# Attention and MLP in one kernel: short transposes and row sums written beside the next unit's scores, and a step that begins with its transposes

## The chip, the cores and the metric

One core of a Trainium2 chip runs the whole program. The metric is device time in microseconds (us), from launch to end; less is better. Engines are named as in the profile: PE (TensorE matmuls), PEld (its weight loads), DVE (VectorE), ACT (ScalarE), POOL (GpSimd), SP (the queue that issues nearly all transfers).

## What is computed

Attention over 4 batches and 8 heads (576 positions, head size 64) with a bias from a tiny network of the distance between positions, then a two-layer network over all 2304 tokens:

```python
scores = q @ k.T / sqrt(64) + bias[head]           # 576 x 576 for each batch and head
attn   = exp(scores - max); attn = attn / (sum(attn) + 1e-9)
x      = (attn @ v), heads side by side            # 2304 x 512
h      = maximum(x @ w_in, 0)                       # 2304 x 2048
out    = (s * h * h + b) @ w_out                    # 2304 x 512
```

All data is fp32. Scores and the two layers are made of three products each of rounded parts (hi and lo).

## The kernel before

**Stages.** First the bias of all heads is computed (until about 57 us), then attention (to about 340 us), then the MLP. The change touches attention and the seam to the MLP.

**Units and steps.** A pair is one head of two batches, x = 0 and 1, held in the two halves of the partitions; there are 16 pairs. A pair has 576 query rows a batch: four units (t = 0 to 3) of 128 rows for both batches, and a fifth (t = 4) with the last 64 rows of both in one tile, so 80 units in all. `step(n)` (L476) is one turn of a software pipeline; p, u = divmod(n, 5). In one turn stand

- **S**, the scores of unit n+2 (`scores`, L214, matmuls L228, row-tiled 64x128 in the first four units of a pair) and `biased` (L237, DVE instruction L242), which subtracts scores and bias and takes the row's minimum, once for each x;
- **T**, the transposes of unit n (`probs_t`, L287): one short one of 128 columns (L307) whose copy is on ACT (L308), then four and four long ones (L298), copied by ACT (L303) and by DVE (L305). For t = 4 they are a short one (L316, two ACT copies L318), the transposed reciprocal row sums (`norm_t`, L270, copy L272) and four long ones (L311, DVE copy L313);
- `expo` (L249), the exponentials of unit n+2 on ACT (L253), with row sums;
- **A**, the output matmuls of the pair before (`av`, L322, matmuls L332, for u = 4 L335, which then scale it on DVE, L340);
- one or two calls of `fill()` (two where u is even), each one more piece of decoding a weight tile. A tile takes five pieces: one on ACT (L372), one on POOL (L374), three on DVE (L376, L379, L382); 24 tiles are decoded here.

`norm(p)` (L263) turns the row sums of a pair into reciprocals (L265, L266) at u = 3.

**What sets the order.** Instructions of each engine run in the order in which this code issues them (`tc.manual_schedule()`). The transfers' queue SP carries at u = 4 the store of the transposed sums (L278, L280), at u = 0 their broadcast load (L285), and at n = LAST - 4 the loads of the MLP's first tokens (L410).

**Buffers.** PSUM tiles of scores come from `ps_s` (two tiles of two banks, one tile for each x; only columns 0 to 287 of each bank of 512 are written), those of transposes from `ps_t` (two tiles of one bank). Three tiles each are there for the biased scores (`tt`) and for the exponentials (`pr`).

**The seam.** At the end (L612 to L618) the last steps are woven with the splitting of the first tokens into hi and lo (`split_x`, L415: ACT L418, then DVE L419) and the first MLP blocks (`expand`, L421, matmuls L429).

## Time and profile before

| what | us |
|---|---|
| runs shown | 747.33, 746.71, 746.08 (median 746.71) |
| span of the profiled execution, first to last instruction | 747.1 |
| the profiled execution's own time, launch to end | not among the times shown; the span stands for it |
| PE busy | 716.6 (96%) |
| DVE, ACT, POOL busy | 429.3 (57%), 363.5 (49%), 186.3 (25%) |
| mean granted PE clock | 0.993 |

Read the page so: PE's busy time is nearly the span, but matmuls overlap, so a busy PE can still wait between two of them; the waits show in the weight loads (PEld) and in the starts of matmuls. The shares of DVE and ACT are means over stages: both work far more in attention than in the MLP.

### The profile page before, as it was taken

The numbers are of one execution on the slowest core, as the hardware profiler recorded it, in microseconds if no ns is written. First come the engines' busy times: TensorE is split into PE (matmuls) and PEld (weight loads), VectorE is DVE, ScalarE is ACT, GpSimd is POOL, SyncE is SP. The second block draws the span as 40 slices with busy tenths as digits, with TensorE's granted clock in tenths as the row PEclk, the third lists the DMA queues.
The fourth block names the chain that finished last, engine by engine and source line by source line (L and its number), as shares of the span: only waits on it lengthen the run. The fifth ranks groups of instructions, "written<-read, shape, count | busy, mean of one in ns | idle before, by whom it ended". The sixth has DMA issues, their size and how long they took to land.

```text
span 747.1 us, 12023 instructions
## 1 busy us (share of the span) xinstructions
PE 716.6 (96%) x4530; PEld 534.9 (72%) x4530; DVE 429.3 (57%) x794; ACT 363.5 (49%) x756; POOL 186.3 (25%) x194
## 2 busy tenths in 40 slices
PE   8978999899999999969999999999999999999998
PEld 4436666666666666646888888888888888888896
DVE  7976888788888878963288632233332332223332
ACT  7967767576666667653445322232222332222332
POOL 7991534445333234203654100000000000000000
PEclk9999999999999999989999999999999999999999
DMA  5977765556564765351012130000300002000100
GB/s 171 297 205 245 227 204 170 176 156 212 160 215 134 228 214 184 97 176 60 13 57 85 29 114 0 1 1 0 113 1 0 1 1 84 1 0 1 57 1 28
DMA packets 39817, 76.98 MB, mean 103 GB/s; under 512 B 9040, under 2 KB 12368, under 8 KB 39760
## 3 DMA queue, kind: packets, MB, share of 16 engines
q1 hardware_dynamic: 39616, 75.90, 32.4%
q8 instruction: 35, 0.57, 0.3%
q10 hardware_dynamic: 144, 0.33, 0.1%
q14 instruction: 22, 0.18, 0.1%
HBM read 55.45 MB, written 20.13 MB: 101 GB/s over the span
## 4 chain that ended last, share of the span: by engine, by line
PE 81%; issue 3%; POOL 3%; ACT 2%; DVE 1%; DMA 1%; SPq 1%; DVEq 0%; ACTq 0%; POOLq 0%
PE hps L429 27%; PE o L453 27%; PE sps L228 8%; PE xps L332 7%; PE tps L298 7%; PE xps L335 2%; PE tps L307 2%; PE tps L311 1%; POOL kr L204 1%; ACT ptr L318 1%; DMA x<-xt 1%; POOL qr L204 1%; PE tps L270 1%; POOL full L374 0%; PE tps L316 0%
## 5 line engine op out<-in xcount | busy, mean ns | idle before, releaser
L453 PE MATMUL o<-who,gt 128*128 128x512 f32 x576 | 192.5, 393 | 0.0
L429 PE MATMUL hps<-x,whi 128*128 128x512 f32 (+1 forms) x640 | 184.5, 373 | 0.0
L434 DVE SCALAR_TENSOR_TENSOR r<-r,sb 128x512 f32<-128x512 f32 (+1 forms) x80 | 56.7, 708 | 193.2 <-ACT r L433 193.2
L433 ACT ACTIVATE r<-hps 128x512 f32<-128x512 f32 (+1 forms) x80 | 44.4, 555 | 227.5 <-PE hps L429 227.5
L429 PEld LDWEIGHTS hps<-x,whi 128*128 128x128 f32 x640 | 117.5, 189 | 24.1 <-issue 0.4
L453 PEld LDWEIGHTS o<-who,gt 128*128 128x128 f32 x576 | 108.3, 188 | 24.1
L429 PE MATMUL hps<-x,wli 128*128 128x512 f32 (+1 forms) x320 | 119.0, 372 | 0.0
L253 ACT ACTIVATE pr<-tt,mn 128x576 f32<-128x576 f32 x144 | 110.1, 767 | 10.3 <-DVE mn L242 9.7
L453 PE MATMUL o<-wlo,gt 128*128 128x512 f32 x288 | 113.2, 393 | 0.0
L242 DVE CUSTOM_DVE_ANT_0 tt<-sps,bt 128x576 f32<-128x576 f32 x128 | 91.6, 753 | 29.4 <-PE sps L228 24.0
L228 PEld LDWEIGHTS sps<-kr,qr 64*128 64x128 f32 (+1 forms) x864 | 67.8, 185 | 39.6 <-issue 10.1
L228 PE MATMUL sps<-kr,qr 64*128 64x288 f32 (+1 forms) x864 | 88.3, 311 | 5.8 <-POOL kr L204 2.7
L439 DVE SCALAR_TENSOR_TENSOR gt<-r,sb,gt 128x512 fp32r<-128x512 f32 (+1 forms) x80 | 56.3, 704 | 54.0 <-ACT gt L438 54.0
L438 ACT ACTIVATE gt<-r,sb 128x512 fp32r<-128x512 f32 (+1 forms) x80 | 54.4, 680 | 52.2 <-DVE r L434 52.2
L298 PE MATMUL tps<-ident,pr 128*128 128x128 f32 x512 | 77.1, 282 | 0.3 <-ACT ptr L308 0.3
L332 PE MATMUL xps<-pt,vt 128*64 128x288 f32 x512 | 76.5, 421 | 0.0
L429 PEld LDWEIGHTS hps<-x,wli 128*128 128x128 f32 x320 | 60.3, 188 | 11.1
L298 PEld LDWEIGHTS tps<-ident,pr 128*128 128x128 f32 x512 | 57.7, 142 | 11.4 <-ACT ptr L308 11.2
L453 PEld LDWEIGHTS o<-wlo,gt 128*128 128x128 f32 x288 | 54.2, 188 | 11.6
L374 POOL TENSOR_SCALAR full<-full 128x512 f32<-128x512 f32 x32 | 22.6, 705 | 115.1 <-ACT full L372 114.6
L332 PEld LDWEIGHTS xps<-pt,vt 128*64 128x64 f32 x512 | 31.5, 137 | 24.3 <-issue 10.6
L136 PE MATMUL bps<-f,pt__110 128*32 128x512 f32 x288 | 42.8, 599 | 5.3 <-POOL f L119 2.2
(69 smaller groups left out, 748.1 us busy)
## 6 DMA issues: line engine op xcount, KB each, us to landing
bias<-stg SPq DMA_DIRECT2D x36, 288.0 KB
raw<-in_moe_w_in_dram SPq DMA_DIRECT2D x16, 512.0 KB
raw<-in_moe_w_out_dram SPq DMA_DIRECT2D x16, 512.0 KB
bt<-bias SPq DMA_DIRECT2D x7, 1152.0 KB
qt<-in_q_dram SPq DMA_DIRECT2D x16, 320.0 KB
kt<-in_k_dram SPq DMA_DIRECT2D x16, 320.0 KB
vt<-in_v_dram SPq DMA_DIRECT2D x16, 320.0 KB
rb<-rs SPq DMA_DIRECT2D x32, 144.0 KB
```

The source lines that it names most:

```text
L136: nc.tensor.matmul(pb[32 * c:32 * c + 32, 0:512], w2bd, fs[c][0][:, 0:8], start=True, stop=True)
L228: nc.tensor.matmul(o, a, b, start=(i == 0), stop=(i == 2))
L242: nc.vector.tensor_tensor_reduce(tt.rearrange("p (a b) -> p a b", a=2), ps[x][:, :, 0:HALF], bias.rearrange("p (a b) -> p a b", a=2), -1.0 ...
L253: nc.scalar.activation(pr[:, x], tts.pop((n, x)), AF.Exp, bias=mn[:, x:x + 1], scale=-1.0, accum_out=sums[p][:, col:col + 1])
L298: nc.tensor.transpose(ps[:, 128 * kb:128 * kb + 128], pr[:, part, 64 * part + 128 * kb:64 * part + 128 * kb + 128], ident)
L332: nc.tensor.matmul(ps[64 * x:64 * x + 64, hf, 0:HALF], vt[:, 4 * x + kb, :], pt[:, kb, x, c], start=(kb == 0), stop=False)
L429: nc.tensor.matmul(ps[:, 0:n], w[0, g][:, a, fc], xs_t[c, a][:, j, 0:n], start=(i == 0), stop=(i == 3 * KB - 1))
L433: nc.scalar.activation(r, ps[:, 0:n], AF.Relu)
L434: nc.vector.scalar_tensor_tensor(r, r, sb[:, 0:1], r, op0=ALU.mult, op1=ALU.mult)
L438: nc.scalar.activation(hi, r, AF.Identity, bias=sb[:, 1:2])
L439: nc.vector.scalar_tensor_tensor(lo, r, sb[:, 1:2], hi.bitcast(F32), op0=ALU.add, op1=ALU.subtract)
L453: nc.tensor.matmul(os_t[c][i], gt[:, a, tok], w[1, g][:, fo], start=(f == 0 and j == 0), stop=(f == NF - 1 and j == 2))
```

## The change

A step now begins with T, then S, then A. The short transposes no longer take a tile of `ps_t`: they write columns 288 to 415 of the x = 0 score tile of unit n+1 (`spare`), of its first bank, and for t = 4 the row sums go to the same columns of its second bank. Only in the last units, where there is no such tile, a `ps_t` tile is used. `norm_t` becomes `norm_copy`, with its transpose moved up beside the other short one. The exponential of x = 1 of a unit is issued one step later, between the short copy and the first long copy of that step (`later`). `norm(p)` keeps its place behind `biased`, now in the step's second half.

```diff
@@ -266,10 +266,9 @@
         nc.vector.reciprocal(su, su)
         rows[p] = su
 
-    def norm_t(p, ps):
-        nc.tensor.transpose(ps[0:9, 128:256], rows.pop(p), ident)
+    def norm_copy(p, ps):
         rt = sm.tile([9, 128], F32, tag="rt", name="rt", bufs=2)
-        nc.vector.tensor_copy(rt, ps[0:9, 128:256])
+        nc.vector.tensor_copy(rt, ps)
         rts[p] = rt
 
     def norm_store(p):
@@ -284,40 +283,53 @@
         for x in range(2):
             nc.sync.dma_start(out=rbs[p][64 * x:64 * x + 64, :], in_=rs_d[p][x:x + 1, :].broadcast_to([D, S]))
 
-    def probs_t(n, part):
+    def spare(n):
+        if n + 1 < LAST - 1:
+            return units[n + 1][2][0][:, :, HALF:]
+        return ps_t.tile([128, 512], F32, tag="t", name="tps").rearrange("p (a b) -> p a b", a=2)
+
+    def probs_t(n):
         p, t = divmod(n, 5)
         pr = units[n][0]
         if p not in pts:
             pts[p] = (ptp.tile([128, 4, 2, S], F32, tag="pt", name="pt"),
                       ptp.tile([128, S], F32, tag="ptr", name="ptr"))
         pt, ptr = pts[p]
-        ps = ps_t.tile([128, 512], F32, tag="t", name="tps")
         c = slice(128 * t, 128 * t + 128)
-        if t < 4 and part < 2:
-            for kb in range(4):
-                nc.tensor.transpose(
-                    ps[:, 128 * kb:128 * kb + 128],
-                    pr[:, part, 64 * part + 128 * kb:64 * part + 128 * kb + 128], ident)
-            o, i = pt[:, :, part, c], ps.rearrange("p (a b) -> p a b", a=4)
-            if part == 0:
-                nc.scalar.activation(o, i, AF.Copy)
-            else:
-                nc.vector.tensor_copy(o, i)
-        elif t < 4:
-            nc.tensor.transpose(ps[:, 0:128], pr.rearrange("p x j -> p (x j)")[:, 512:640], ident)
-            nc.scalar.activation(ptr[:, c], ps[:, 0:128], AF.Copy)
-        elif part == 0:
+        end = spare(n)
+        if t < 4:
+            nc.tensor.transpose(end[:, 0, 0:128], pr.rearrange("p x j -> p (x j)")[:, 512:640], ident)
+            nc.scalar.activation(ptr[:, c], end[:, 0, 0:128], AF.Copy)
+            later(n + 1)
+            for x in range(2):
+                ps = ps_t.tile([128, 512], F32, tag="t", name="tps")
+                for kb in range(4):
+                    nc.tensor.transpose(
+                        ps[:, 128 * kb:128 * kb + 128],
+                        pr[:, x, 64 * x + 128 * kb:64 * x + 128 * kb + 128], ident)
+                o, i = pt[:, :, x, c], ps.rearrange("p (a b) -> p a b", a=4)
+                if x == 0:
+                    nc.scalar.activation(o, i, AF.Copy)
+                else:
+                    nc.vector.tensor_copy(o, i)
+        else:
+            nc.tensor.transpose(end[0:64, 0, 0:128], pr[:, 0, 512:S], ident)
+            nc.tensor.transpose(end[0:9, 1, 0:128], rows.pop(p), ident)
+            ps = ps_t.tile([128, 512], F32, tag="t", name="tps")
             for kb in range(4):
                 nc.tensor.transpose(
                     ps[:, 128 * kb:128 * kb + 128], pr[:, 0, 128 * kb:128 * kb + 128], ident)
+            for x in range(2):
+                nc.scalar.activation(
+                    ptr[64 * x:64 * x + 64, 512:S], end[0:64, 0, 64 * x:64 * x + 64], AF.Copy)
+            later(n + 1)
+            norm_copy(p, end[0:9, 1, 0:128])
             nc.vector.tensor_copy(
                 pt[:, :, :, 512:S], ps.rearrange("p (a x b) -> p a x b", a=4, x=2))
-        else:
-            nc.tensor.transpose(ps[0:64, 0:128], pr[:, 0, 512:S], ident)
-            for x in range(2):
-                nc.scalar.activation(
-                    ptr[64 * x:64 * x + 64, 512:S], ps[0:64, 64 * x:64 * x + 64], AF.Copy)
-            norm_t(p, ps)
+
+    def later(n):
+        if (n, 1) in tts:
+            expo(n, 1)
 
     def av(p, kb, hf):
         h, b0 = pairs[p]
@@ -477,6 +489,8 @@
         p, u = divmod(n, 5)
         m = n + 2
         cur = 0 <= n < LAST
+        if cur:
+            probs_t(n)
         if ok(m, 0):
             scores(m)
             biased(m, 0)
@@ -484,13 +498,8 @@
             biased(m, 1)
         if cur and u == 3:
             norm(p)
-        if cur:
-            for part in (2, 0, 1) if u < 4 else (1, 0):
-                probs_t(n, part)
         if ok(m, 0):
             expo(m, 0)
-        if ok(m, 1):
-            expo(m, 1)
         if p >= 1:
             av(p - 1, u, 0)
             av(p - 1, u, 1)
@@ -549,7 +558,7 @@
         26: ((load_bias, 0, 2, 3),),
         33: ((scores, 0), (biased, 0, 0), (expo, 0, 0), (biased, 0, 1)),
         35: ((expo, 0, 1), (scores, 1), (biased, 1, 0),
-             (expo, 1, 0), (biased, 1, 1), (expo, 1, 1), (load_w, *early[0]), (load_w, *early[1]),
+             (expo, 1, 0), (biased, 1, 1), (load_w, *early[0]), (load_w, *early[1]),
              (load_q, 2), (load_k, 2), (load_v, 1)),
     }
     for st in range(STEPS):
```

Three places show the order that results; "waits" names the semaphores (engine counters or transfers) that an instruction waits for.

PE, from A of a step with u = 3 to the transposes of the next pair's u = 0, somewhere in the middle of attention; before:

```order
L332 MATMUL xps<-pt,vt 64x288 x4
L228 MATMUL sps<-kr,qr 128x288 [waits DVE_49] x2
L228 MATMUL sps<-kr,qr 128x288 x10
L316 MATMUL tps<-ident,pr 64x128 [waits Activation_49]
L270 MATMUL tps<-ident,su 9x128 [waits DVE_49,Activation_49]
L311 MATMUL tps<-ident,pr 128x128 [waits DVE_49]
L311 MATMUL tps<-ident,pr 128x128 x3
L335 MATMUL xps<-ptr,vt 128x288 x2
L228 MATMUL sps<-kr,qr 128x288 [waits DVE_49] x2
L228 MATMUL sps<-kr,qr 128x288 x10
L307 MATMUL tps<-ident,pr 128x128 [waits DVE_49]
```

and now:

```order
L344 MATMUL xps<-pt,vt 64x288 x4
L316 MATMUL sps<-ident,pr 64x128 [waits DVE_49]
L317 MATMUL sps<-ident,su 9x128 [waits DVE_49]
L320 MATMUL tps<-ident,pr 128x128 [waits Activation_49]
L320 MATMUL tps<-ident,pr 128x128 x3
L228 MATMUL sps<-kr,qr 128x288 [waits PE_49]
L228 MATMUL sps<-kr,qr 128x288 [waits DVE_49]
L228 MATMUL sps<-kr,qr 128x288 x10
L347 MATMUL xps<-ptr,vt 128x288 x2
L301 MATMUL sps<-ident,pr 128x128 [waits DVE_49,Activation_49]
```

The transposed sums (in: su) no longer wait for ACT, but stand right behind A of the step in which DVE makes the reciprocals, with the scores behind them. The short transpose (L301) now waits for DVE as well as ACT.

ACT, in a step in which a decode piece falls; before:

```order
L308 ACTIVATE ptr<-tps 128x128 [waits PE_49]
L303 ACTIVATE pt<-tps 128x4x128 [waits PE_49]
L253 ACTIVATE pr,su<-tt,mn 128x576 [waits DVE_49] x2
L372 ACTIVATE full_986<-raw 128x512 [waits DMAHW0_49]
L308 ACTIVATE ptr<-tps 128x128 [waits PE_49]
L303 ACTIVATE pt<-tps 128x4x128 [waits PE_49]
```

and now (two steps):

```order
L302 ACTIVATE ptr<-sps 128x128 [waits PE_49]
L253 ACTIVATE pr,su<-tt,mn 128x576 [waits DVE_49]
L312 ACTIVATE pt<-tps 128x4x128 [waits PE_49]
L253 ACTIVATE pr,su<-tt,mn 128x576 [waits DVE_49]
L384 ACTIVATE full_985<-raw 128x512 [waits DMAHW0_49]
L302 ACTIVATE ptr<-sps 128x128 [waits PE_49]
L312 ACTIVATE pt<-tps 128x4x128 [waits PE_49]
```

One exponential moved behind the short copy; the decode piece (L384) still stands ahead of the short copy of the next step.

DVE, from the reciprocals at u = 3 on; before:

```order
L265 TENSOR_SCALAR su<-su 128x9 [waits Activation_49]
L266 RECIPROCAL su<-su 128x9 [waits DVE_49]
L305 COPY pt<-tps 128x4x128 [waits PE_49]
L242 ISA tt,mn<-sps,bt 128x576 [waits PE_49]
L242 ISA mn 128x1
L242 ISA tt,mn<-sps,bt 128x576 [waits PE_49,Activation_49]
L242 ISA mn 128x1
L272 COPY rt<-tps 9x128 [waits DMAHW4_49,DMAHW3_49,PE_49]
```

and now:

```order
L265 TENSOR_SCALAR su<-su 128x9 [waits Activation_49]
L266 RECIPROCAL su<-su 128x9 [waits DVE_49]
L271 COPY rt<-sps 9x128 [waits DMAHW3_49,DMAHW4_49,PE_49,Activation_49]
L327 COPY pt<-tps 128x8x64 [waits PE_49]
L242 ISA tt,mn<-sps,bt 128x576 [waits PE_49]
L242 ISA mn 128x1
L242 ISA tt,mn<-sps,bt 128x576 [waits PE_49]
L242 ISA mn 128x1
```

The copy of the sums now waits for ACT too, and stands ahead of the biased scores of its step.

## Rows read from the trace of the kernel before

**Rows 1.** Windows view, two stretches: us, busy time of each engine, PEclk, DMA, GB/s
```profile
125.00:150.00 25.00, 23.03 (x178) 15.66 (x176) 20.81 (x44) 14.64 (x37) 10.02 (x10) 0.93 0.59 186
325.00:350.00 25.00, 18.98 (x97) 12.48 (x94) 8.54 (x15) 8.19 (x18) 1.56 (x2) 0.86 0.48 161
```

**Rows 2.** Waits view, 60 to 330 us: who waited for whom, total us, times, longest
```profile
PEld tps L298 <- ACT ptr L308: 11.2, 63, 0.5
PEld tps L270 <- ACT ptr L318: 10.9, 15, 0.7
...
PE sps L228 <- POOL kr L204: 2.7, 4, 1.3
```

**Rows 3.** Timeline, one step, PE: start us, us, engine, line, op
```profile
183.20 1.07 PE L228 MATMUL sps<-kr,qr 64*128 64x288 f32 x12
...
184.36 1.19 PE L298 MATMUL tps<-ident,pr 128*128 128x128 f32 x8
...
185.48 1.19 PE L332 MATMUL xps<-pt,vt 128*64 128x288 f32 x8
...
186.60 1.07 PE L228 MATMUL sps<-kr,qr 128*128 128x288 f32 x6
```

**Rows 4.** Timeline, end of a step with u = 3 and its u = 4
```profile
191.04 0.76 DVE L242 CUSTOM_DVE_ANT_0 tt<-sps,bt 128x576 f32<-128x576 f32 x1 [1.18 <-issue]
...
192.61 0.22 DVE L266 RECIPROCAL su<-su 128x9 f32<-128x9 f32 x1
...
193.25 1.06 PE L228 MATMUL sps<-kr,qr 64*128 64x288 f32 x12
...
194.24 0.30 PE L316 MATMUL tps<-ident,pr 128*64 128x128 f32 x1
...
194.34 0.76 DVE L242 CUSTOM_DVE_ANT_0 tt<-sps,bt 128x576 f32<-128x576 f32 x1 [0.38 <-PE sps L228]
194.57 0.44 ACT L318 ACTIVATE ptr<-tps 64x64 f32<-64x64 f32 x2 [0.82 <-PE tps L316]
...
195.07 0.28 PE L270 MATMUL tps<-ident,su 128*9 128x128 f32 x1 [0.53 <-ACT ptr L318]
...
195.19 0.60 PE L311 MATMUL tps<-ident,pr 128*128 128x128 f32 x4
...
195.62 1.14 PE L335 MATMUL xps<-ptr,vt 128*128 128x288 f32 x4
...
195.70 0.27 DVE L272 COPY rt<-tps 9x128 f32<-9x128 f32 x1
...
195.91 0.67 DVE L313 COPY pt<-tps 128x512 f32<-128x512 f32 x1
...
196.79 0.76 DVE L340 TENSOR_TENSOR rb<-xps,rb 128x576 f32<-128x576 f32 x1 [0.22 <-PE xps L335]
```

**Rows 5.** Lines view, shapes apart, whole span: line, engine, op, count, busy us, mean ns
```profile
L253 ACT ACTIVATE pr<-tt,mn 128x576 f32<-128x576 f32 x144 | 110.1, 767 | 10.3 <-DVE mn L242 9.7
...
L379 DVE SCALAR_TENSOR_TENSOR full<-raw,full 128x512 uint32<-128x512 uint32 x32 | 31.7, 989 | 0.6
...
L376 DVE TENSOR_SCALAR full<-full 128x512 uint32<-128x512 uint32 x32 | 29.5, 921 | 2.3 <-POOL full L374 2.1
...
L382 DVE SCALAR_TENSOR_TENSOR full<-raw,full 128x512 uint32<-128x512 uint32 x32 | 22.9, 717 | 0.6
...
L372 ACT ACTIVATE full<-raw 128x512 f32<-128x512 f32 x32 | 21.1, 660 | 0.0
```

**Rows 6.** Timeline, the seam from attention to the MLP
```profile
334.02 0.69 DVE L419 TENSOR_TENSOR x<-x 128x512 fp32r<-128x512 f32 x1 [1.30 <-ACT x L418]
334.37 0.09 PEld L270 LDWEIGHTS tps<-ident,su 128*9 128x9 f32 x1 [6.21 <-ACT ptr L318]
...
335.40 2.12 PE L335 MATMUL xps<-ptr,vt 128*128 128x288 f32 x4
...
341.02 3.13 PE L332 MATMUL xps<-pt,vt 128*64 128x288 f32 x24
```

## The prediction

> **What bounds the kernel now.** I read the busy times by stretch first, then who waits for whom, then one step in order of time, then the seam. In attention PE sets the pace: in a middle stretch it is busy 23.03 of 25 us, but DVE is close behind with 20.81, while late in the program there is little of DVE [rows 1]. So a wait taken off PE is worth its full length only as long as DVE and ACT can follow. The waits view shows two waits of PE that the change aims at: the fifth long transpose waits for the short copy on ACT, 63 times, 11.2 us by the weight loads, and the transposed sums wait for the copies L318, 15 times, 10.9 us [rows 2]. One step reads so [rows 3]: scores start at 183.20, the long transposes at 184.36, the output at 185.48, the next scores at 186.60. The period is 3.40 us, of which A is 1.12.
>
> **What the change removes.** Both short products leave the transposes' two buffers, so the second four need no copy on ACT.
> - Long transposes: a wait is 11.2/63 = 0.18 us by the weight loads. Part of it lies beside the matmul that still runs; hidden by one transpose (0.43/4 = 0.11, from 195.19 to 195.62 [rows 4]) it would be worth 0.07, hidden by nothing 0.18. I take 0.15, nearer to the latter because the eight take 1.12 where twice the four would take 0.86: 63 x 0.15 = **-9.5** (between -4.4 and -11.2).
> - Sums: L316 to L270 takes 0.83 (194.24 to 195.07), L270 to the next 0.12 [rows 4]; the difference of 0.71 goes, in 15 pairs: **-10.7**. The 16th is at the seam, below.
>
> A full step would then be 3.25: S 1.00, A 1.12, T 1.13. No matmul is added, and the same instructions run on ACT and DVE; what S, T and A cost by themselves is only moved, and the shape changes of PE's tile between them stay as many. SP's transfers keep their places in the step; none is passed.
>
> **What it adds.** Four waits, each worked from the start of a step's scores as time 0; the DVE bias of these scores starts at 1.09 (193.25 to 194.34 [rows 4]).
> - *Reciprocals.* At u = 3 DVE takes 1.79 from the first bias to the end of the reciprocal (191.04 to 192.61 + 0.22), so they are ready at 2.88. PE now wants them after S (0.99), A (1.12) and L316 (0.12), at 2.23. Wait 0.65, 16 times: **+10.4** [rows 3, 4]. Before, T stood ahead of A and one step later, so that this was covered.
> - *The sums' copy.* The scores behind it need the bank back: transposed sums 0.28, the two ACT copies 0.44, DVE's copy 0.27, with hand-overs of 0.06 (195.01 to 195.07) some 1.1 in all. PE has 0.12 + 0.43 and a shape change of about 0.1 to do. Wait 0.45, 16 times: **+7.2** [rows 4]. The old cover, A, now stands behind the scores.
> - *The bank that DVE reads.* The first short transpose of a step writes into the tile whose bias DVE computes, and so waits for it. DVE is free at 2.45 (195.70 - 193.25), then come the decode pieces F, then the copy of the long transposes (0.67), then the bias, wanted at 3.25 + 1.09 = 4.34: spare 1.22. The bias ends at 4.34 + 0.76 = 5.10, and PE wants it at 3.25 + 2.12 = 5.37: spare 0.27, so 1.49 together [rows 4]. Two pieces in a row are on DVE for 0, 0.92, 1.91, 1.71 or 0.72 [rows 5]. At u = 0 the excess over 1.49 is 0.42 and 0.22, 0.13 in the mean of five; at u = 4 the scaled output (0.76) comes on top, excess 0.19, 1.18 and 0.98, mean 0.47; at u = 2 there is only one bias to compute and nothing is over. 15 x 0.60 = **+9.0** (0 if DVE's pieces run at the short ends of their times, 18 if they meet the long ones each time).
> - *The short copy behind a decode piece.* The bias ends at 1.85, the exponential (0.77 [rows 5]) at 2.67, the short copy at 2.95, scores follow at 3.25: spare 0.25 with a hand-over. A decode piece of ACT of 0.66 between them [rows 5] makes 0.41, 24 times 9.8; half of these fall in steps already held up by one of the other waits: **+4.9** (0 to 9.8).
>
> The moved exponential itself costs nothing: it runs while PE transposes, and its unit is wanted a step later; without that cover it would be 0.77 on the path.
>
> **The seam.** Before, the last L270 waits 6.21 us for two ACT copies queued behind the splitting of the first tokens, and then PE runs slow: four output matmuls take 2.12 from 335.40 where they took 1.14 [rows 4, 6]; the clock in that stretch is 0.86, which is a part at the lower of its two levels, 1.2 GHz, after the idle time [rows 1]. Now both short transposes and the long ones go ahead of those copies. The first MLP block can start on the tokens that are there; the last split ends at 334.71, then DVE copies sums (0.27) and transposes (0.67) and scales (0.76): 336.4, when the output steps that started at 341.02 can start: **-4.5** (0 if the tokens land later, -6.3 with nothing behind the split).
>
> Scores wait for POOL's rounded keys 2.7 us before [rows 2]; a slower pace gives POOL time, I take half: **-1.3**.
>
> Sum: -9.5 - 10.7 + 10.4 + 7.2 + 9.0 + 4.9 - 4.5 - 1.3 = **+5.5 us**. The span of the profiled execution is 747.1, 0.4 above the median of the runs shown (746.7) and inside their spread; I put the sum on the median: **752.2 us**.
>
> A rule of the Trainium skill speaks against this change: PSUM — Partial Sum Buffer, section "PSUM bank collisions raise a hardware error", says to guard PSUM by bank and group of 32 partitions, not by address, since two engines in one bank collide even in different columns. The trace agrees: before, L270 waits 0.53 for copies that read other columns of its bank [rows 4]. By columns alone the bank's wait would be nothing and the sum -3.5; by the rule it is +5.5, and the new order shows L301 waiting for DVE.
>
> **The rivals.**
> 1. *DVE and ACT keep up* (faster). If the decode pieces lie so that the short transpose finds its bank read and the copy stands free, the last two of the four waits are 0: 752.2 - 13.9 = 738.3. It decides at F = 1.49 us of DVE pieces after u = 0, and 0.73 after u = 4. For it: DVE's pieces vary, and ACT has slack (14.64 of 25 [rows 1]). Against: their mean is 0.72 to 0.99 [rows 5], and DVE's 20.81 of 25 leaves little. Chance 0.15.
> 2. *Gains and losses cancel.* The moved waits cost about what the removed ones did and the seam gives little, or the change does not shorten PE's path because the waits were beside running matmuls: 747 within 1.5. Chance 0.11.
> 3. *The clock falls more often.* In the stretch from 125 to 150 us the granted clock is 0.93, below full, in a part of attention in which scores waited for POOL; so PE that pauses can lose its full clock. A stretch like it costs 25 x 0.07 = 1.75 us. With four more of them: 752.2 + 7 = 759.2. Against: the sums' waits of 0.53 us [rows 4] recur in every pair, and this stretch, which shows the lower clock, is one with a wait for POOL of up to 1.3 [rows 2]. Chance 0.12.
>
> On the third, the skill's page TensorE: Matmul & The Clock Gate, section "HAM oscillation — how this bites in real kernels", says that waits between bursts of matmuls let the clock fall each time, so that the cost repeats. No row here shows waits of the new lengths doing so.
>
> **How the numbers follow.** The forecast itself, slower by some 3 to 9 us, has 0.62. The first rival lies on the other side, so the range reaches towards it: the lower end takes the bank's and the decode piece's waits at a third of their price and is 743; the upper end adds the decode piece in full (4.9) and a seam that gives a third (3), 760. Outside are most of the first rival and the end of the third. About 0.2% (1.5 us) is what a measurement of this kernel can tell from no change. Faster: the first rival and a little of the second, 0.18. Same: most of the second, 0.08. Slower: the forecast and the third, 0.74.
>
> **What the profile of the changed kernel would show.** Right: the waits of long transposes for the short copy gone; PE waiting at L317 for the reciprocal some 0.65 in each pair, at the scores behind it for the sums' copy or ACT, at L301 for the bias in steps after two decode pieces; pairs that take over 17 us, where five steps of 3.40 made 17.0 at most; no idle time of 6 us at the seam, and the clock full there. Wrong: pairs of 16.4 or less, L301 never waiting, or L317 finding its sums ready; or long idle stretches of PE with a clock below full in the middle of attention.

## The result and the profile after

The changed kernel takes 759.44 us (median of 4 runs, 756.43 to 760.17), the kernel before, run beside it, 747.02 (4 runs, 746.08 to 747.41): a ratio of 1.0149, with a 95% interval of 1.013 to 1.0168, so about 11 us slower where +5.5 was forecast. Three of its runs show a mean granted clock of 0.990 to 0.993, the one of 756.43 shows 0.998. The profiled execution spans 757.1 us, 10.0 more than the one of before.

Where these 10.0 us came from is read by the starts of the same instructions in the two profiled executions (us):

| instruction on PE | before | after | later by | in this stretch |
|---|---|---|---|---|
| second unit's scores, L228 | 56.61 | 59.11 | 2.50 | +2.50 |
| pair 0, the output matmuls of u = 4 (first L335, now L347) | 88.97 | 94.75 | 5.78 | +3.28 |
| pair 13, the same | 314.56 | 325.64 | 11.08 | +5.30 |
| first MLP matmul (L429, now L441) | 336.92 | 342.34 | 5.42 | -5.66 |
| last pair's u = 4 over, third MLP block begins | 349.06 | 354.56 | 5.50 | +0.08 |
| first output matmul of the MLP (L453, now L465) | 352.07 | 360.46 | 8.39 | +2.89 |
| 49th of them | 374.49 | 384.50 | 10.01 | +1.62 |

From there to the start of PE's last matmul both take 368.54 us. Thirteen pairs of attention make only half of the loss; the rest lies at the start, in the first pair, and behind the seam.

**The middle of attention.** The waits view of the changed kernel, 60 to 330 us (who waited for whom, total us, times, longest):

```profile
PEld sps L317 <- DVE su L266: 12.5, 15, 1.1
PE sps L317 <- DVE su L266: 9.7, 15, 0.9
...
PE sps L301 <- DVE mn L242: 8.3, 13, 1.0
...
PEld sps L228 <- DVE rt L271: 4.5, 15, 0.4
PEld sps L228 <- ACT ptr L302: 3.9, 18, 0.3
...
PEld sps L228 <- POOL kr L204: 0.9, 2, 0.7
PE sps L228 <- POOL kr L204: 0.4, 1, 0.4
```

The two waits of [rows 2] that the change aimed at are gone, and all four that the prediction named stand in their place: the sums' transpose for the reciprocals, the short transpose for the bias that reads its tile (8.3 us of matmuls, of which 4.9 fall in the first pair, before 88 us), the scores for the sums' copy and for the short copy. The wait for POOL's keys fell from 2.7 us of matmuls to 0.4.

The same step as in [rows 4], on PE, with ACT's and DVE's part (start us, us, engine, line, and in brackets the idle time before and what ended it):

```profile
195.70 0.32 PE L301 MATMUL sps<-ident,pr 128*128 128x128 f32 x1
195.86 1.04 PE L307 MATMUL tps<-ident,pr 128*128 128x128 f32 x8
196.82 1.06 PE L228 MATMUL sps<-kr,qr 64*128 64x288 f32 x12
197.81 1.19 PE L344 MATMUL xps<-pt,vt 128*64 128x288 f32 x8
198.93 0.30 PE L316 MATMUL sps<-ident,pr 128*64 128x128 f32 x1
199.57 0.21 DVE L266 RECIPROCAL su<-su 128x9 f32<-128x9 f32 x1
199.84 0.28 PE L317 MATMUL sps<-ident,su 128*9 128x128 f32 x1 [0.61 <-DVE su L266]
199.96 0.60 PE L320 MATMUL tps<-ident,pr 128*128 128x128 f32 x4
200.16 0.45 ACT L323 ACTIVATE ptr<-sps 64x64 f32<-64x64 f32 x2 [0.48 <-PE sps L317]
200.49 1.53 PE L228 MATMUL sps<-kr,qr 64*128 64x288 f32 x12
200.63 0.28 DVE L271 COPY rt<-sps 9x128 f32<-9x128 f32 x1 [0.30 <-ACT ptr L323]
201.95 1.24 PE L347 MATMUL xps<-ptr,vt 128*128 128x288 f32 x4
```

A step without a wait takes 3.23 (195.70 to 198.93): T 1.12, S 0.99, A 1.12. The reader should compare L316 to L317, 0.91 here, with L316 to L270 in [rows 4], 0.83: the sums' wait of before was not removed, it was exchanged for one on another engine. Behind it the scores, 0.99 in steps without a wait, take 1.46 to the next line: the copy L323 of the first short transpose waits until L317 has written the other bank of the tile, and DVE's copy of the sums then waits for L323.

**The first pair.** The timeline of the first steps of attention, where no pair stands before and so there is no A:

```profile
59.76 0.93 PE L228 MATMUL sps<-kr,qr 64*128 64x288 f32 x8
61.64 0.30 PE L301 MATMUL sps<-ident,pr 128*128 128x128 f32 x1 [0.95 <-DVE mn L242]
...
64.84 0.30 PE L301 MATMUL sps<-ident,pr 128*128 128x128 f32 x1 [1.04 <-DVE mn L242]
```

The short transpose follows the scores directly and waits about 1 us in each step for the bias that reads its tile.

**The seam.** The timeline of the changed kernel:

```profile
340.26 1.14 PE L347 MATMUL xps<-ptr,vt 128*128 128x288 f32 x4
341.66 2.63 ACT L430 ACTIVATE x<-x 128x512 fp32r<-128x512 f32 x4 [3.35 <-DMA x<-xt]
342.34 0.50 PE L441 MATMUL hps<-x,whi 128*128 128x512 f32 x1 [0.94 <-ACT x L430]
344.93 0.27 DVE L271 COPY rt<-tps 9x128 f32<-9x128 f32 x1
...
359.55 0.76 DVE L352 TENSOR_TENSOR rb<-xps,rb 128x576 f32<-128x576 f32 x1 [3.74 <-DMA rb<-rs]
360.46 0.60 PE L465 MATMUL o<-who,gt 128*128 128x512 f32 x1 [2.73 <-DVE rb L352]
```

and its chain of waits (start us, us, what) between 344.93 and 359.55:

```profile
347.09 8.54 DMA rs<-rt
...
356.25 3.18 DMA rb<-rs
```

PE no longer idles 6.21 us, and its four matmuls take 1.14 instead of 2.12 [rows 6]. But the last pair's sums are now copied at 344.93, behind the splitting of the first tokens; their way through memory and back takes until 359.5, and the first output matmul, whose PSUM the scaling L352 must leave, waits for it. In this execution the clock then drops. The windows view (us, busy time of PE, PEld, DVE, ACT, POOL, PEclk, DMA, GB/s), two stretches that answer to [rows 1], the stretch behind this wait, and the one at the start:

```profile
125.00:150.00 25.00, 22.97 (x180) 16.02 (x181) 20.69 (x48) 14.55 (x39) 7.85 (x8) 1.00 0.68 206
330.00:355.00 25.00, 22.66 (x145) 14.64 (x141) 13.19 (x26) 12.50 (x29) 1.06 (x1) 1.00 0.48 162
...
53.00:60.20 7.20, 6.56 (x51) 3.41 (x53) 1.44 (x4) 2.60 (x5) 5.21 (x5) 0.53 0.63 162
360.00:364.00 4.00, 3.54 (x9) 2.80 (x10) 2.10 (x3) 0.72 (x1) 2.34 (x2) 0.58 0.08 18
```

The full clock at the seam was forecast and is there; 0.58 behind it, most of the stretch at the lower of the two levels (1.2 GHz), was not. That the clock falls there is not certain: six profiles show PE idle for 2.0 to 2.7 us before this matmul. In four of them (the changed kernel, a_seam, a_first, a_nodec) the 48 matmuls behind it take 23.9 to 24.0 us, in a_pst and a_x1 22.4 and 22.5, as in the kernel before.

### The profile page after: what moved, and what is told of

Same layout as the page of the kernel before. It is cut to its first block, busy times and chain, and to the rows that moved or that the text cites. A ratio compares the mean times of both kernels' runs of the same rounds, so it can differ in the third digit from the quotient of the medians.

```text
span 757.1 us, 12070 instructions
## 1 busy us (share of the span) xinstructions
PE 719.2 (95%) x4530; PEld 540.7 (71%) x4530; DVE 426.9 (56%) x794; ACT 357.0 (47%) x756; POOL 184.9 (24%) x194
## 4 chain that ended last, share of the span: by engine, by line
PE 73%; DMA 10%; DVE 9%; issue 4%; ACT 2%; SPq 1%; POOL 1%; DVEq 0%; ACTq 0%; POOLq 0%
PE o L465 27%; PE hps L441 25%; PE sps L228 8%; DMA rs<-rt 5%; PE tps L307 4%; PE xps L344 4%; DVE tt L242 3%; PE bps L136 3%; DMA bias<-stg 2%; PE sps L301 1%; DMA bt<-bias 1%; DVE full L391 1%; PE xps L347 1%; DVE rb L352 1%; DMA raw<-in_moe_w_in_dram 1%
## 5 line engine op out<-in xcount | busy, mean ns | idle before, releaser
L465 PE MATMUL o<-who,gt 128*128 128x512 f32 x576 | 193.6, 395 | 2.7 <-DVE rb L352 2.7
L441 PE MATMUL hps<-x,whi 128*128 128x512 f32 (+1 forms) x640 | 183.7, 371 | 1.2 <-ACT x L430 0.9
L441 PEld LDWEIGHTS hps<-x,whi 128*128 128x128 f32 x640 | 116.9, 188 | 25.9 <-ACT x L430 1.4
L465 PEld LDWEIGHTS o<-who,gt 128*128 128x128 f32 x576 | 109.1, 189 | 27.5 <-ACT whi L405 3.1
L441 PE MATMUL hps<-x,wli 128*128 128x512 f32 (+1 forms) x320 | 118.7, 371 | 0.0
L465 PE MATMUL o<-wlo,gt 128*128 128x512 f32 x288 | 113.9, 395 | 0.0
L228 PE MATMUL sps<-kr,qr 64*128 64x288 f32 (+1 forms) x864 | 98.9, 315 | 2.8 <-ACT stg L143 0.7
L228 PEld LDWEIGHTS sps<-kr,qr 64*128 64x128 f32 (+1 forms) x864 | 72.9, 187 | 20.9 <-issue 7.4
L441 PEld LDWEIGHTS hps<-x,wli 128*128 128x128 f32 x320 | 60.1, 188 | 10.8
L307 PE MATMUL tps<-ident,pr 128*128 128x128 f32 x512 | 66.6, 273 | 0.2 <-ACT ptr L302 0.2
L465 PEld LDWEIGHTS o<-wlo,gt 128*128 128x128 f32 x288 | 54.5, 189 | 11.7
L314 DVE COPY pt<-tps 128x512 f32<-128x512 f32 x64 | 44.0, 687 | 20.3 <-PE tps L307 19.6
L136 PE MATMUL bps<-f,pt__110 128*32 128x512 f32 x288 | 44.6, 624 | 5.2 <-POOL f L119 2.3
```

Of the source, the lines that this page charges most:

```text
L136: nc.tensor.matmul(pb[32 * c:32 * c + 32, 0:512], w2bd, fs[c][0][:, 0:8], start=True, stop=True)
L228: nc.tensor.matmul(o, a, b, start=(i == 0), stop=(i == 2))
L307: nc.tensor.transpose(ps[:, 128 * kb:128 * kb + 128], pr[:, x, 64 * x + 128 * kb:64 * x + 128 * kb + 128], ident)
L441: nc.tensor.matmul(ps[:, 0:n], w[0, g][:, a, fc], xs_t[c, a][:, j, 0:n], start=(i == 0), stop=(i == 3 * KB - 1))
L465: nc.tensor.matmul(os_t[c][i], gt[:, a, tok], w[1, g][:, fo], start=(f == 0 and j == 0), stop=(f == NF - 1 and j == 2))
```

## The experiments

Times are medians; each kernel was compared with the kernel before on its own chip (747.1 to 748.4 us), and its distance to the changed kernel is the difference of their ratios to before, times 747. "Period" is the mean time of a pair: from the first L347 (L335 in before) of pair 0 to that of pair 13, divided by 13. For the kernel before it is 17.35 us in its profile, where nine pairs without a disturbance take 16.87 to 16.91, 16.89 in the middle; for the changed kernel it is 17.76.

### Where do 13.9 us of the forecast come from: the decode pieces

```diff
 def decode_w(kind, g, i):
     if g < 3:
-        full = fulls[g][:, kind, i]
+        for _ in range(5):
+            yield
+        w_full[kind, g, i] = fulls[g][:, kind, i]
+        return
...
+    for g in (2, 1):
+        nc.gpsimd.memset(fulls[g], 0.01)
```

The same edit in the changed kernel (a_nodec) and in the kernel before (b_nodec): the decoding of 24 weight tiles is left out and constants stand in their place, so that the outputs are not those of the reference.

> The changed kernel without the decoding of the weight tiles of parts 0 to 2 (24 tiles; constants stand in their place, so the first layers' results are not the reference's): the pieces of decoding leave ACT, DVE and POOL during attention, all else stays. Theory (the forecast's third and fourth added wait are made by these pieces): 9.0 + 4.9 = 14 us come off, 745 us, between 742 and 749, and the pairs in attention take 16.8 or less, while the waits for the reciprocals and for the sums' copy stay. Rival (the added waits come from the order of the step itself, the pieces only fill idle time): less than 5 us come off, 754 or more.

> The kernel before, with the same decoding left out (the same constants in its place). Theory: before the change the steps have cover for the pieces, so no more than 5 us come off (742 to 747), most of them waits for POOL's rounded keys; the difference of the two kernels without decoding is then about 0 to 5 us where it is 11 with it. Rival: the pieces cost the kernel before as much as the changed one (some 14 us, 733), and the difference stays at 11.

Measured: 747.28 us (741.55 to 749.53) for the changed kernel without decoding, ratio 0.9981 (0.9959 to 1.0003), 12.5 below it; 746.42 (744.88 to 748.03) for the kernel before without it, a ratio of 0.9977 (0.9962 to 0.9993) to before, some 1.7 us. (This second gain is partly given back in the first pair, where POOL writes the constants and a part runs at the lower clock: it is 3.6 us longer.) The periods are clearer: 16.86 and 16.92. The waits view of a_nodec, 60 to 330 us:

```profile
PE sps L317 <- DVE su L266: 9.4, 15, 0.7
...
PEld sps L228 <- DVE rt L271: 4.5, 15, 0.3
PE sps L301 <- DVE mn L242: 4.3, 5, 1.0
```

The waits for reciprocals and for the sums' copy stay as they were, to 0.3 us; the waits for the short copy on ACT (3.9 us in the changed kernel) are gone, and those of L301 for the bias fall from 13 to 5, behind the first pair from 8 (3.4 us) to 1 (0.3 us). So the two groups of added waits are told apart: without pieces of decoding the change wins 0.06 us a pair (16.92 - 16.86); the pieces cost the changed kernel 0.90 a pair (17.76 - 16.86), where (9.0 + 4.9)/16 = 0.87 was forecast, and the kernel before 0.43 (17.35 - 16.92), most of it waits for POOL's keys.

How the 0.90 divides is read from PE's starts in the 13 pairs of the period (us):

| from ... to | changed | a_nodec | more | forecast, for 13 pairs |
|---|---|---|---|---|
| A to the next T: the short transpose's wait for the bias | 77.35 | 72.83 | 4.52 | 7.8 |
| T to S | 75.94 | 76.01 | -0.07 | 0 |
| S to A: the scores' wait for the short copy | 77.60 | 70.39 | 7.21 | 4.2 |

The sum agrees, its two parts do not: the bias costs 0.35 us a pair (0.60 forecast), the short copy 0.55 (0.9 us in all of that are waits for POOL's keys). Of the 39 steps with u = 0, 2 or 4 there are 18 in which the scores take 1.33 us or more to the next line and not 0.99. Two of them wait for POOL's keys; in 16 a decode piece stands on ACT just ahead of the short copy. They pay 0.35 to 0.44 us each (forecast 0.41), but 16 of the 21 pieces in these pairs do so, where half was forecast. One of the 16, on the timeline of the changed kernel:

```profile
225.01 0.66 ACT L384 ACTIVATE full<-raw 128x512 f32<-128x512 f32 x1
225.45 1.49 PE L228 MATMUL sps<-kr,qr 64*128 64x288 f32 x12
225.57 0.26 ACT L302 ACTIVATE ptr<-sps 128x128 f32<-128x128 f32 x1
225.89 0.82 PEld L228 LDWEIGHTS sps<-kr,qr 64*128 64x128 f32 x11 [0.25 <-ACT ptr L302]
```

The decode piece on ACT stands ahead of the short copy, and the scores wait for that copy.

### The tile that is read, not the columns

```diff
-            return units[n + 1][2][0][:, :, HALF:]
+            return units[n + 1][2][-1][:, :, HALF:]
```

> The changed kernel with the spare columns in the score tile of x = 1 of unit n+1 (the one whose bias DVE computes last) in place of x = 0. Nothing else is changed. Theory (PE waits at the short transpose for DVE's reading of the bank, not of the columns): the bias of x = 1 ends 0.76 to 0.9 us later, so with a spare of 0.3 in a step without excess each of some 45 steps waits 0.3 to 0.5 longer: 10 to 22 us more than the changed kernel, 769 to 781. Rival (the wait hangs on the columns, or there is slack beyond what was counted): within 3 us of the changed kernel, 757 to 762.

Measured: 776.34 us (774.86 to 777.47), ratio 1.0374 (1.0343 to 1.0405), 16.8 above the changed kernel; period 18.90. The waits view, 60 to 330 us, and the starts of two steps on the timeline:

```profile
PE sps L301 <- DVE mn L242: 26.0, 42, 1.7
```

```profile
199.20 0.30 PE L301 MATMUL sps<-ident,pr 128*128 128x128 f32 x1 [0.61 <-DVE mn L242]
...
203.09 0.30 PE L301 MATMUL sps<-ident,pr 128*128 128x128 f32 x1 [0.61 <-DVE mn L242]
```

The columns are the same 288 to 415, free in either tile; only the tile whose bias DVE reads last is another. 26.0 us of matmul waits stand where 8.3 stood (behind the first pair 20.2 and 3.4). What a short transpose waits for is the end of a reader of other columns of its tile. Whether bank or whole tile makes the wait, this run cannot tell: the bias reads both banks of the tile. The step shown above speaks for the whole tile, since there L323 waits 0.48 us for L317 and L271 0.30 for L323, each for a neighbour in the other bank; no run tests it.

### The order alone

```diff
 def spare(n):
-        if n + 1 < LAST - 1:
-            return units[n + 1][2][0][:, :, HALF:]
```

> The changed kernel's order alone: the short transposes and the sums go to a tile of the transposes' buffers as before, all else stays as changed. Theory (the waits of the long transposes for the short copy and of the sums for theirs return, and now both stand ahead of the scores, on the path): 63 x 0.2 to 0.3 us and 16 x 0.5 to 0.7 us more, less 9 us for the bank that DVE reads, which is no longer shared; the exponential that now stands between the short copy and the first long one comes on top where the third tile waits for it: 5 to 25 us above the changed kernel, 764 to 784. Rival (the order is what costs, and the columns bring nothing): within 3 us of the changed kernel, 756 to 762.

Measured: 778.08 us (2 runs), ratio 1.04 (1.0368 to 1.0432), 18.8 above the changed kernel; period 19.10. Its waits view, 60 to 330 us:

```profile
PEld tps L305 <- ACT ptr L300: 42.2, 57, 1.6
```

The wait for the short copy, 11.2 us in [rows 2], is 42.2 in the new order (by the weight loads too, 57 times). The theory holds. The order alone is about 30 us slower than the kernel before; the columns take 18.8 of that back, which is less than the order costs. Whether the columns could be had in another order was not tried.

### Both exponentials at once

```diff
         if ok(m, 0):
             expo(m, 0)
+        if ok(m, 1):
+            expo(m, 1)
...
-            later(n + 1)
```

> The changed kernel, but both exponentials of a unit are issued together, as before; nothing is postponed. The forecast took the postponing at nothing and said that without cover it would be 0.77 us on the path. Theory (the short copy, on which the next scores wait, then stands behind both exponentials; the bias of the second ends 0.68 later and it takes 0.77): the scores of full steps wait 0.3 us and more, 48 times and over, so 10 to 25 us more than the changed kernel, 769 to 784. Rival (ACT has slack enough): within 3 us of the changed kernel.

Measured: 775.35 us (774.82 to 776.32), ratio 1.038 (1.036 to 1.04), 17.3 above the changed kernel; period 18.90. Rows of its waits view, 60 to 330 us:

```profile
PEld sps L228 <- ACT ptr L302: 16.5, 33, 1.1
PEld sps L301 <- DVE mn L242: 15.1, 29, 1.1
```

With the second exponential ahead of the short copy the scores wait four times as long for that copy. The moved exponential is a needed part of the order; that it is free where the change puts it is not shown by this run.

### The sums behind the output matmuls

```diff
-            nc.tensor.transpose(end[0:9, 1, 0:128], rows.pop(p), ident)
...
-            norm_copy(p, end[0:9, 1, 0:128])
...
             av(p - 1, u, 1)
+        if cur and u == 4:
+            norm_t(p)
```

> The changed kernel, but the transpose of the row sums and its copy stand behind the output matmuls of their step, in a tile of the transposes' own buffers. Theory (PE waits for the reciprocal in every pair, 12.5 us by the weight loads, and the scores behind it wait for the copy of the sums, 4.5 us): 7 to 13 us less than the changed kernel, 746 to 752. Rival (DVE sets the pace of a pair, so what is taken off here turns up as a longer wait of the short transposes for the bias): less than 4 us.

Measured: 751.89 us (750.09 to 754.77), ratio 1.0067 (1.0046 to 1.0087), 6.1 below the changed kernel, between what theory and rival expected; period 17.49. A row of its waits view, 60 to 330 us:

```profile
PEld tps L312 <- DVE rt L271: 10.1, 15, 0.9
```

The wait of L317 is gone, but its successor is already there: the long transposes of the next step find one of the two tiles held by the sums' copy. 0.27 us a pair is left (17.76 - 17.49, 3.5 us in 13 pairs), and the first pair, which shares the L317 wait, is 1.4 shorter. At the seam two things nearly cancel: up to the first MLP matmul 3.8 us more (20.51 against 16.70; the sums' transpose again waits for two ACT copies behind the split tokens), behind it 4.5 less (the first output matmul follows the third MLP block in 3.01 us, as in before, not in 5.90, and the next stretch takes 22.42 instead of 24.04). So the wait for the reciprocals was real, but moving the sums gives back only what the two tiles allow: neither text was right about the size.

### The first pair in the old order

```diff
-        if cur:
+        if cur and n >= 5:
             probs_t(n)
...
+        if cur and n < 5:
+            probs_t(n)
```

(with `spare` taking a `ps_t` tile for n < 5.)

> The changed kernel with the first pair (5 steps) in the order of before: scores, then transposes in the transposes' own buffers; all later steps as changed. Theory (in the first pair no output matmuls lie between scores and transposes, so each short transpose waits about 1 us for the bias of the scores just made): 2 to 4 us less than the changed kernel, and the waits of 1.3 us between scores and short transposes from 60 to 78 us gone. Rival (the slow start is the clock at its lower level from 53 to 60 us and nothing else): within 1 us.

Measured: 753.7 us (751.55 to 756.43), ratio 1.0087 (1.0067 to 1.0107), 4.6 below the changed kernel by the ratios. From the second unit's scores to L347 of pair 0 it takes 31.71 us; the changed kernel 35.64, the kernel before 32.36; the period stays at 17.76. The windows view from 60 to 80 us, of the changed kernel and of this one:

```profile
60.00:80.00 20.00, 13.33 (x123) 10.82 (x123) 12.52 (x31) 13.24 (x37) 0.00 (x0) 0.99 0.89 287
```

```profile
60.00:80.00 20.00, 18.87 (x157) 13.96 (x153) 14.89 (x37) 15.84 (x43) 3.05 (x4) 1.00 0.89 289
```

PE is busy 13.33 us of 20 in the one, 18.87 in the other. So the first pair alone costs some 4 us, a little more than expected.

### The seam, twice

```diff
-    for work in (att, xsp, xsp, xsp, xsp, att, h0, ...
+    for work in (att, att, xsp, xsp, xsp, xsp, h0, ...
```

> The changed kernel with one difference at the seam: the last unit's transposes and copies are issued before the splitting of the first tokens, not behind it. Theory (the sums of the last pair are copied late, their store and broadcast load take some 12 us, and the first matmul of the second layer waits for the scaled output behind them, 3.1 us, after which the clock stands at its lower level): 3 to 5 us less than the changed kernel, so about 754 to 756, and no idle time of 3 us before the first output matmul of the MLP. Rival (the wait there is set by the tokens or by the weights, and the loss sits in the pairs alone): within 1.5 us of the changed kernel.

Measured: 757.19 us (755.44 to 762.03), ratio 1.0142 (1.0115 to 1.0169): the same as the changed kernel, and the theory missed. A row of SP on its timeline points to the reason:

```profile
339.90 4.18 SPq L277 DMA_DIRECT2D rs<-rt  x1
```

The sums were copied earlier, but the issue of their store took 4.18 us instead of 0.49, with the issues of four weight loads of 512 KB each (L371) just ahead of it in the queue. So these were moved as well:

```diff
-    for e in late[0:4]:
-        load_w(*e)
...
+    lw = map(lambda e: load_w(*e), late[0:4])
+    for work in (att, att, lw, lw, lw, lw, xsp, xsp, xsp, xsp, h0, ...
```

> The changed kernel with the second of the last attention steps ahead of the splitting of the first tokens, and the loads of four weight tiles of 512 KB behind the store of the last sums. Theory: the store of the sums then issues at once, the broadcast row sums arrive before the first output matmul of the last pair, the wait of about 3 us in front of it and the slower clock behind it go: 4 us below the changed kernel (3 to 6), 753.5 to 756.5. Rival: the store's chain is late for another cause (the loads of the first tokens, or the late weight loads then hold up something else), and the time stays above 757.

Measured: 755.35 us (754.8 to 757.15), ratio 1.0101 (1.008 to 1.0122), 3.6 below the changed kernel. The store and the first output matmul now:

```profile
343.85 0.48 SPq L277 DMA_DIRECT2D rs<-rt  x1
...
359.53 0.47 PE L465 MATMUL o<-who,gt 128*128 128x512 f32 x1 [1.43 <-DVE rb L352]
```

The store issues in 0.48 us, the wait falls from 2.73 to 1.43, and the output matmuls behind it run at full clock (22.45 us for 48 of them, not 24.04). The theory holds, though the wait did not go altogether: in the chain of waits the load of the sums back (`rb<-rs`) now takes 5.74 us, where it took 3.18.

### All four faults undone

a_sums, a_first and a_seam2 together.

> The changed kernel with the four faults found so far undone: the sums transposed behind the output matmuls, the first pair in the order of before, the second attention step ahead of the splitting of the first tokens, the late weight loads behind the store of the sums. Theory: 6.1 + 4.6 + 4.1 us less than the changed kernel if the parts add up, less some 2 us because the sums moved and the seam mended both end the wait at the first output matmul: 13 us less, 746 (744 to 749), no better than the kernel before. Rival (the parts hide each other's waits): more than 18 us less, 741 or below, faster than before.

Measured: 747.76 us (747.05 to 749.35, 12 runs), ratio 0.9998 (0.9982 to 1.0013), 11.3 below the changed kernel. Mended at these four places, the changed order is worth as much as the order of before (period 17.49 against 17.35), as the theory had it.

### What the change aimed at, in the order of before

b_sums puts the sums' transpose of the kernel before behind the output matmuls, in a tile of its own; b_best takes the seam of a_seam2 as well.

```diff
-            norm_t(p, ps)
...
             av(p - 1, u, 1)
+        if cur and u == 4:
+            norm_t(p)
```

> The kernel before with the sums' transpose behind the output matmuls alone. Theory: 5 to 9 us below the kernel before; the rows of the wait for the copies of L318 go and the pairs take 16.3 us instead of 16.89. Rival: the next short transpose waits for its tile instead, the pairs stay at 16.8 to 16.9 and the time within 2 us of the kernel before.

> The kernel before with two things only: the sums are transposed behind the output matmuls of the step with u = 4 ahead of which they stood (in a tile of their own of the transposes' buffers), and the seam takes the second attention step ahead of the splitting of the first tokens, with the late weight loads behind the store of the last sums. Theory (the two waits of before that the change aimed at, the sums' 0.7 us in each pair and the 6 us at the seam, can be had without its order): 15 x 0.5 to 0.7 us for the pairs less what the tile's new owner waits, and 3 to 5 us at the seam: 9 us below the kernel before (6 to 14), about 739. Rival (the sums' wait reappears at the long transposes, as it did with the changed kernel's sums moved, where 10.1 us stood at the transposes that wait for the sums' copy): only the seam is left, 743 to 746.

Measured: b_sums 740.2 us (739.06 to 741.99), ratio 0.9896 (0.9876 to 0.9915), 7.8 below before; **b_best 736.45 us** (735.72 to 736.94), ratio 0.9842 (0.9824 to 0.9861), 11.8 below before and 23 below the changed kernel. The timeline of b_best at u = 4 and after it:

```profile
156.29 0.30 PE L317 MATMUL tps<-ident,pr 128*64 128x128 f32 x1
156.43 0.60 PE L312 MATMUL tps<-ident,pr 128*128 128x128 f32 x4
156.87 1.14 PE L335 MATMUL xps<-ptr,vt 128*128 128x288 f32 x4
157.84 0.27 PE L271 MATMUL tps<-ident,su 128*9 128x128 f32 x1
158.04 1.06 PE L228 MATMUL sps<-kr,qr 64*128 64x288 f32 x12
...
159.64 1.09 PE L299 MATMUL tps<-ident,pr 128*128 128x128 f32 x8 [0.28 <-DVE rt L273]
```

L317 to the long transposes L312 takes 0.14 where L316 to L311 took 0.95 (0.83 of it to L270) [rows 4]: no transpose between them needs the first one's copies any more. The sums stand a whole A behind their reciprocals, and the scores between them and the long transposes cover most of their copy. An undisturbed pair takes 16.23 instead of 16.89, and the period is 16.83 instead of 17.35. Both forecasts of the theory, 5 to 9 us and 6 to 14, hold.

## Why the prediction came out as it did

The time, 759.4, is inside the range (743 to 760), and slower was the likelier side; the likeliest value, 752.2, was too small by 7 us, more than the change it forecast. By its own steps:

- **Removed waits and the first two added ones: right.** A step of 3.23 (forecast 3.25). L317 waits 9.7/15 = 0.65 us (forecast 0.65), the scores behind it take 1.46 instead of 0.99, 0.47 more (forecast 0.45; by the weight loads 4.5/15 = 0.30). Without decode pieces the change gains 0.06 us a pair where (20.2 - 17.6)/16 = 0.16 was forecast: that the sums' wait only moves to another engine was the heart of the forecast.
- **The bank and the decode piece on ACT: right as mechanisms, and in the sum by luck,** 0.90 us a pair against 0.87. The bank's "15 x 0.60" was too large, 0.35 in the traces: behind the pieces of u = 4, where 0.47 was forecast, only 0.16 came, behind those of u = 0 0.10 (0.13). The short copy's +4.9 was too small, 7.2 in 13 pairs: the price of one wait was right, but 16 of 21 pieces are paid for, not half of them. In a_x1, where the columns stay and only the tile changes, L301's waits grow from 8.3 to 26.0 us. The Trainium skill, PSUM — Partial Sum Buffer, section "PSUM bank collisions raise a hardware error", has the rule by which the wait is there at all: PSUM is guarded by bank and partitions, not by address. By columns alone a_x1 would have cost nothing; its 16.8 us agree with the rule, though they do not tell a bank from the whole tile.
- **The moved exponential at nothing: not contradicted.** Undoing it costs 17.3 us. In the waits view of the changed kernel, 60 to 330 us, PE's matmuls wait for no exponential, its weight loads once, 1.2 us in the first pair.
- **The first pair, put at nothing without a reason: a step that failed.** The bank's wait was costed for "15 x 0.60", in the pairs with A between S and T. In the first pair there is no A, so the cover is missing in every step. The profile shows +3.28 us there; a_first takes back 4.6 (3.9 of them in this stretch of its profile).
- **The seam, "-4.5": the term that failed.** What it was made of came: -5.66 up to the first MLP matmul, and full clock. But the step "when the output steps that started at 341.02 can start" stopped at the scaling of the pair before. The last pair's own sums, behind the split tokens, were not followed to their store, their load and L352: +2.89, and in this execution +1.62 for the clock. The stretches make -5.66 + 0.08 + 2.89 + 1.62 = -1.1 together, where -4.5 was forecast. a_seam2 takes back 3.6.
- **POOL, "I take half: -1.3": too small.** Thirteen pairs of before took 225.59 us, 6.0 more than 13 x 16.89. By the weight loads 4.2 of these were waits for POOL's keys; most of the rest went where PE ran at a granted clock of 0.59 from 137.0 to 141.2 us. In the changed kernel 0.9 of the first are left and the clock is 1.00 from 90 to 330 us: 13 x (17.76 - 16.89) = 11.3 us are added by the four waits, less what the removed ones gave, and the table shows 5.3. Why the changed order frees the scores from POOL's keys was not tried; a_combo2 has that relief too (0.9 us by the weight loads), b_best has not (4.9).
- **The start, not counted:** 2.50 us before any transpose of attention, with the clock at 0.53. Of the fourteen profiles three show it, all of kernels with the changed order; no run isolates its cause.

So two terms, the first pair (+3.3 in the profile, at nothing in the sum) and the seam (-1.1 for -4.5), were too kind to the change, and POOL's was too hard on it. From +5.5 to the 10.0 of the profile the seam adds 3.4, the first pair 3.3 and the start 2.5; the pairs give back 4.7, since they came to 5.3 where all the other terms made 10.0 (for 15 or 16 pairs, of which two lie in the stretch of the seam). With a_first's 4.6 and a_seam2's 3.6 taken off, 759.4 would be 751.2, near the forecast; but that is partly luck, since the start and POOL's term, both missed, lie on opposite sides.

Of the rivals the third, the clock, names almost the time measured (759.2), but not its mechanism: the mean clock is 0.993 in both profiles, and the pairs, where it was placed, run at 1.00. The lower clock is elsewhere, at the start and behind the seam's wait, 2.5 and 1.6 of the 10.0 us. The page that was set beside it, the Trainium skill's TensorE: Matmul & The Clock Gate, section "HAM oscillation — how this bites in real kernels", speaks of waits for transfers between bursts of matmuls, each of which lets the clock fall. The waits of 0.65 us in the pairs here are shorter and of another kind, and the clock does not fall at them. The first rival, that DVE and ACT keep up, is what a_nodec makes true, and even then the changed kernel is no faster than before. The second falls: gains and losses did not cancel.

## What to carry to other kernels

A wait that ends on one engine's copy is not removed by giving the result another home, if the new home is read by a busier engine, or if the producer of the operand is itself late: look first for a place in the order where both the operand is long ready and the next owner comes late (here behind A, 11.8 us together with the seam, by a few lines). Cost a moved step in the first and the last turn of the pipeline too, where its cover is missing. At a seam, follow the last item to its last transfer: a store of a few KB that stands behind large loads in one queue can hold up what comes 15 us later.

## What was not expected of the hardware

- The issue of a store of a few KB took 4.18 us with four loads of 512 KB just ahead on the same queue (a_seam), and 0.48 where these stand behind it (a_seam2). In the changed kernel, where the store comes 7 us after them, it took 0.49. From the start of the first issue to the landing the sums' four stores took 8.54 us in the changed kernel and 8.26 in a_seam2, with the token loads around them.
- Eight profiles have the first pair in the changed order; four of them (a_expo, a_x1, a_seam2, a_pst) show the lower clock in parts of that pair, as in this window of a_x1:

```profile
64.00:85.00 21.00, 15.08 (x98) 12.09 (x98) 9.65 (x23) 9.82 (x26) 0.00 (x0) 0.68 0.92 306
```

  Of the six with the old order there, one does (b_nodec, 3.4 us). Why some executions show it and others do not was not tested.
